# Order of a fused attention and feed-forward kernel: the first 24 heads' output transposes planned after the reciprocals of the sums

## The chip, the cores and the metric

One core of a Trainium2 chip runs the kernel. The metric is the device time of one execution in microseconds (us). The engines are TensorE (PE, its weight loads apart as PEld), VectorE (DVE), ScalarE (ACT), GpSimd (POOL) and SyncE (SP), which issues most of the transfers. Products are made in fp32 or in fp32r, a form of fp32 that the engine takes in one go.

## The reference

Four batches of 12 heads, 448 positions and 64 columns go through attention with a soft cap; the heads' outputs side by side are normalised and go through a feed-forward block with a residual:

```python
scores = scale * np.matmul(q, k.transpose(0, 1, 3, 2))
scores = cap * np.tanh(scores / cap)
scores = scores - np.max(scores, axis=-1, keepdims=True)
attn = np.exp(scores)
attn = attn / (np.sum(attn, axis=-1, keepdims=True) + 1e-09)
return np.matmul(attn, v).astype(np.float32)
...
mu = np.mean(x, axis=-1, keepdims=True)
var = np.mean((x - mu) ** 2, axis=-1, keepdims=True)
xn = (x - mu) / np.sqrt(var + 1e-06) * g_ln
ch = np.maximum(xn @ w_ch1, 0.0) @ w_ch2
return (x + ch).astype(np.float32)
```

## The kernel before, in words

The kernel doesn't write its instructions in the order in which they run. It describes the work as operations (`add`), each with an engine, an assumed cost, the buffers that it reads and writes and a due time. From the reads and writes `Order.add` makes the dependencies. `Order.emit` then plays the program through with the assumed costs: whenever an engine is free it takes, of the operations whose dependencies are met and whose buffers can be had, the one due first, gives it its buffers and writes its instructions. What comes out is a fixed list of instructions for each engine. On the chip every engine goes through its list in order, and its waits follow from the tiles that an instruction really touches; what was only named in `reads` orders the list and makes no wait on the chip.

PSUM has eight banks in four tiles of two banks (named `two_225` to `two_228` in the program; `two` in the profile). A score block of the first heads takes a whole tile, everything else takes one bank of it. Which tile a thing gets is settled by the same play-through, so another order also means other tiles.

Heads come in quads of four (`quad`, L498); the first 24 heads (`LEAD`) are six quads, and the feed-forward work of their tokens only begins when 12 heads are done. A quad is made of these parts:

- Scores, L723: key blocks of 128 against 448 queries, two heads at a time, one in each half of the array's rows (64*128). ACT takes the tanh (L768) and, for three blocks together, the exponential (L776). The last 64 keys are L749 (64*64), their exponential L784.
- Values, L552: the exponentials times V, two heads side by side in columns (128*64), into the accumulators `pos`, one bank for each pair of heads; L559 (64*64) adds the last keys.
- Sums of the exponentials: DVE adds key blocks (L575, L577) and PE sums over partitions with a matrix of ones (L636, L640, 128*32).
- The `pos` are copied to SBUF, the `ot` tiles (L603 through `copy`: L611 on DVE for the first eight heads, L609 on ACT after them), and so are the sums (`ss`, L656).
- `finish` (L647): PE transposes the sums (L662, four of 128x128), DVE adds a small number and takes the reciprocal (L665, L668, tile `r`). PE transposes the outputs (L676): four token tiles, two transposes each, each tile in a bank `pf`. DVE multiplies each by the reciprocals into the token layout (L686), which frees the bank.

After 12 heads, tokens are normalised (L858 to L891), transposed (L899), rounded into a high and a low part (L904 on ACT, L908 on DVE), and the feed-forward products begin (L1019 to L1021 and L1048 to L1050, fp32r, whole array); from some 490 us on the remaining tokens follow in blocks of 512 (L1237 to L1240, L1330 to L1332).

In the kernel before, the transposes L676 name only the two `ot` tiles, so they can be planned as soon as those are copied; the multiplies name `pf` and `r`.

Of the kernel before, what the change touches and what calls it, by code (L numbers as in the profile page):

```python
# [33 lines left out]
LEAD = 24  # L34
# [113 lines left out]
class Order:  # L148
# [9 lines left out]
    def add(self, engines, fn, reads=(), writes=(), allocs=(), due=0.0, dma=0, after=(), lag=0.0):  # L158
        op = Op()
        (op.engine, op.cost), = engines.items()  # L160
        op.fn, op.due, op.dma, op.lag, op.seq = fn, due, dma, lag, len(self.ops)
        deps = set(after)
        for k in reads:
            deps.update(self.writer.get(k, ()))
        for k in writes:
            deps.update(self.writer.get(k, ()))
            deps.update(self.readers.get(k, ()))
        for k in writes:
            self.writer[k], self.readers[k] = [op], []
        for k in reads:  # L170
            self.readers.setdefault(k, []).append(op)
        deps.discard(op)
        op.left, op.outs, op.ready, op.end, op.wait, op.after = len(deps), [], 0.0, None, None, deps
        for d in deps:
            d.outs.append(op)
        bufs = {k[0] if isinstance(k, tuple) else k: 0 for k in (*reads, *writes, *allocs)}
        op.bufs = [b for b in bufs if isinstance(b, Buf)]
        for b in op.bufs:
            self.wide += b.wide and not b.users
            b.users += 1  # L180
            op.ready = max(op.ready, b.since)
        self.ops.append(op)
        return op
# [196 lines left out]
class Program:  # L380
# [25 lines left out]
    def buf(self, pool, tag, shape, dtype, bufs=1):  # L406
        size = 1
        for x in shape[1:]:
            size *= x
        kinds, tags = (GENERAL_KINDS, GENERAL_TAGS) if self.general else (KINDS, TAGS)  # L410
        if tag in tags:
            kind, n = tags[tag]
            self.limits[pool, tag] = n
            bufs, size = kinds[kind]
        else:
            kind = tag
        self.places[pool, kind] = bufs
        b = Buf(pool, kind, tag, shape, dtype)
        self.sizes[pool, kind] = max(size, self.sizes.get((pool, kind), 0))
        return b  # L420
# [226 lines left out]
    def finish(self, i, pairs, ps, due, late):  # L647


        nc, add, buf = self.nc, self.add, self.buf  # L650
        b, h0 = divmod(i, H)
        part = HEADS[-(i < FRONT)]
        due += PLAN["fin"] if h0 + GROUP < H else 0
        ss, d0 = self.out_tile("ss", i, late)
        add({part["ss"]: dict(A=ACTP(S), V=VEC2(S))[part["ss"]]}, lambda e: self.copy(
            e, ss.ap[:, d0:d0 + S], ps.ap[:, :S]), reads=[ps], writes=[(ss, 0)], due=due)  # L656
        pr = buf("ps", "f", [128, 512], F32)
        r = buf("small", "r", [128, NK + 1, GROUP], F32, 2)

        def turn(e):  # L660
            for j in range(NK + 1):
                nc.tensor.transpose(pr.ap[:, j * 128:j * 128 + 128], ss.ap[:, j * 128:j * 128 + 128], self.ident)  # L662

        add({"T": 440}, turn, reads=[(ss, 0), (ss, 2)], writes=[pr], due=due)
        add({"V": 210}, lambda e: nc.vector.tensor_scalar(  # L665
            r.ap, pr.ap.rearrange("p (j c x) -> p j c x", j=NK + 1, c=GROUP)[:, :, :, 0], self.eps, None,
            op0=ALU.add), reads=[pr], writes=[r], due=due)
        add({"V": 220}, lambda e: nc.vector.reciprocal(r.ap, r.ap), writes=[r], due=due)  # L668
        W = GROUP * D
        cols = slice(h0 * D, h0 * D + W)  # L670
        for j, tl, p in self.token_tiles(b):
            pf = buf("ps", "f", [128, 512], F32)

            def turn(e, j=j, pf=pf):
                for c, ot in enumerate(pairs):
                    nc.tensor.transpose(pf.ap[:, c * 128:c * 128 + 128], ot.ap[:, j * 128:j * 128 + 128], self.ident)  # L676

            add({"T": len(pairs) * 110}, turn, reads=[(o, x) for o in pairs for x in (0, 2)] + [r] * self.general, writes=[pf], due=due)
            m = p.stop - p.start
            rows = lambda ap: ap.rearrange("p (h d) -> p h d", d=D)  # L680
            if tl < NA:
                writes, dst = [(self.home(tl)[0], tl, h0)], lambda tl=tl, p=p: self.x(tl)[p, cols]
            else:
                st = buf("att", "stage", [128, W], F32)
                writes, dst = [st], lambda st=st, p=p: st.ap[p]
            add({"V": VEC2(W)}, lambda e, j=j, p=p, m=m, dst=dst, pf=pf: nc.vector.tensor_tensor(  # L686
                out=rows(dst()), in0=rows(pf.ap[p, :W]), in1=r.ap[p, j].unsqueeze(2).to_broadcast([m, GROUP, D]),
                op=ALU.mult), reads=[pf, r], writes=writes, due=due)
            if tl >= NA:
                add({"V": 330}, lambda e, dst=dst, tl=tl, p=p: nc.vector.bn_stats(  # L690
                    self.stats.ap[p, tl % SLOTS, h0 // GROUP], dst()), reads=writes,
                    writes=[(self.stats, tl % SLOTS, h0 // GROUP, p.start)], due=due)
                add({"S": 550}, lambda e, dst=dst, tl=tl, p=p: nc.sync.dma_start(out=self.xd[tl][p, cols], in_=dst()),
                    reads=writes, writes=[("xd", tl, (h0, p.start))], due=due, dma=128 * W * 4)
# [883 lines left out]
```

## Time and profile before

| | |
|---|---|
| three runs | 857.07, 857.84 and 858.79 us, median 857.84 |
| the profiled execution | 857.77 us, of which its span 856.0 us |
| mean granted TensorE clock | 0.998 |
| busy share of the span | PE 99%, PEld 83%, DVE 82%, ACT 60%, POOL 18% |
| chain that ended last | PE 95%, ACT 2%, DVE 1% |

The span goes from the first to the last instruction. A PE row of the timeline gives the start of a stretch of like instructions, its length, and how many there are; an fp32 product in a part of the array counts as two instructions there. The ends of matmuls are modelled and overlap the next stretch, so what a stretch costs is read from its start to the start of the next one.

### The profile page before, as it was taken

How to read it: one execution, taken by the hardware profiler on the slowest of the kernel's cores; microseconds unless marked ns; L12 is line 12 of the kernel's file. 1: busy time of each engine (PE TensorE's matmuls, PEld its weight loads, DVE VectorE, ACT ScalarE, POOL GpSimd, SP SyncE). 2: the span in 40 equal slices, each digit the busy share in tenths (PEclk: the TensorE clock that was granted, in tenths of full speed). 3: DMA queues.
4: the chain of work that ended last, by engine and by line, in shares of the span. 5: the costliest groups of instructions: out<-in, count | busy, mean ns of one | idle time of the engine just before them, and what ended most of it. 6: DMA issues, size and time to landing. Idle time of an engine off the chain costs nothing.

```text
span 856.0 us, 12856 instructions
## 1 busy us (share of the span) xinstructions
PE 845.8 (99%) x4700; PEld 706.4 (83%) x4700; DVE 701.7 (82%) x1157; ACT 511.9 (60%) x795; POOL 152.1 (18%) x198
## 2 busy tenths in 40 slices
PE   8999999999999999999999999999999999999997
PEld 5344477979879799799799989998988998999897
DVE  2689798878789878787689878888888888788896
ACT  6887877644654647354436646756575666566550
POOL 0134231111112111111110001223113212312210
PEclk9999999999999999999999999999999999999999
DMA  9597766665675774654562344798878888787984
GB/s 230 138 251 212 197 179 176 186 204 161 184 221 167 221 210 168 184 169 128 179 254 102 102 143 83 164 180 156 169 159 155 165 169 159 139 191 157 181 220 152
DMA packets 55579, 148.96 MB, mean 174 GB/s; under 512 B 7378, under 2 KB 20178, under 8 KB 55506
## 3 DMA queue, kind: packets, MB, share of 16 engines
q1 hardware_dynamic: 41328, 113.43, 44.8%
q0 software_dynamic: 12096, 33.04, 22.8%
q10 hardware_dynamic: 2082, 1.58, 0.6%
q8 instruction: 39, 0.64, 0.3%
q14 instruction: 34, 0.28, 0.1%
HBM read 87.46 MB, written 60.56 MB: 173 GB/s over the span
## 4 chain that ended last, share of the span: by engine, by line
PE 95%; ACT 2%; DVE 1%; issue 0%; POOL 0%; DVEq 0%; ACTq 0%
PE two L1237 7%; PE two L1330 7%; PE two L1240 7%; PE two L1332 7%; PE two L1331 7%; PE two L1238 7%; PE two L1019 6%; PE two L1048 6%; PE two L1050 6%; PE two L1049 6%; PE two L552 6%; PE two L1021 6%; PE two L1020 6%; PE two L723 6%; PE two L676 1%; PE two L636 1%
## 5 line engine op out<-in xcount | busy, mean ns | idle before, releaser
L1347 POOL DMA_DIRECT2D out_dram<-x x84 | 73.4, 998 | 314.6 <-ACT x L1338 227.2
L1338 ACT ACTIVATE x<-two 128x384 f32<-128x384 f32 x168 | 79.6, 487 | 35.6 <-PE two L1332 27.0
L1237 PE MATMUL two<-X,q 128*128 128x512 f32 x252 | 98.9, 392 | 1.2 <-ACT y L1254 1.2
L1019 PE MATMUL two<-hA,q 128*128 128x384 f32 x288 | 99.8, 347 | 0.0
L1240 PE MATMUL two<-X,q 128*128 128x512 f32 x252 | 98.8, 392 | 0.0
L1238 PE MATMUL two<-X,q 128*128 128x512 f32 x252 | 98.6, 391 | 0.0
L1342 DVE TENSOR_TENSOR x<-two,x 128x384 f32<-128x384 f32 x144 | 76.9, 552 | 26.3 <-PE two L1332 22.7
L1048 PE MATMUL two<-w,hh 128*128 128x384 f32 x288 | 98.3, 341 | 0.0
L1050 PE MATMUL two<-w,hl 128*128 128x384 f32 x288 | 97.2, 337 | 0.0
L1049 PE MATMUL two<-w,hh 128*128 128x384 f32 x288 | 97.1, 337 | 0.0
L1021 PE MATMUL two<-hA,q 128*128 128x384 f32 x288 | 96.9, 337 | 0.0
L1020 PE MATMUL two<-lA,q 128*128 128x384 f32 x288 | 96.8, 336 | 0.0
L951 POOL TENSOR_SCALAR raw<-raw 128x768 f32<-128x768 f32 x48 | 49.5, 1031 | 227.9 <-ACT c L947 213.6
L1330 PE MATMUL two<-w,hop 128*128 128x384 f32 x264 | 89.1, 338 | 0.0
L1332 PE MATMUL two<-w,hop 128*128 128x384 f32 x264 | 88.9, 337 | 0.0
L1331 PE MATMUL two<-w,hop 128*128 128x384 f32 x264 | 88.9, 337 | 0.0
L768 ACT ACTIVATE e<-two,sc 128x448 f32<-128x448 f32 (+1 forms) x108 | 75.0, 758 | 20.1 <-PE two L723 20.1
L1053 DVE TENSOR_TENSOR x<-two,x 128x384 f32<-128x384 f32 x144 | 76.2, 548 | 12.4 <-PE two L1050 12.1
L488 ACT ACTIVATE w<-c 128x768 fp32r<-128x768 f32 x38 | 32.1, 845 | 60.3 <-DVE c L956 22.9
L1019 PEld LDWEIGHTS two<-hA,q 128*128 128x128 f32 x288 | 54.1, 188 | 10.9 <-issue 7.1
L776 ACT ACTIVATE e<-e,capt 128x1344 f32<-128x1344 f32 (+1 forms) x35 | 61.1, 1770 | 0.3
L552 PE MATMUL two<-e,v 128*64 128x448 f32 x288 | 59.2, 547 | 1.1 <-ACT e L776 0.8
(179 smaller groups left out, 1852.1 us busy)
## 6 DMA issues: line engine op xcount, KB each, us to landing
raw<-in_w_dram SPq DMA_DIRECT2D x48, 768.0 KB, 5.0
out_dram<-x POOLq DMA_DIRECT2D x84, 384.0 KB, 7.2
kept<-c SPq DMA_DIRECT2D x47, 384.0 KB, 5.5
d<-in_kq_dram SPq DMA_DIRECT2D x48, 224.0 KB, 5.7
d<-kept SPq DMA_DIRECT2D x23, 384.0 KB, 3.2
c<-kept SPq DMA_DIRECT2D x23, 384.0 KB, 7.4
v<-in_v_dram SPq DMA_DIRECT2D x24, 227.5 KB, 5.8
x<-out_dram SPq DMA_DIRECT2D x13, 384.0 KB, 5.1
```

The costliest lines, as they stand in the source:

```text
L1019: nc.tensor.matmul(ps.ap[:, :n], lhsT=w1h.ap[:, wc], rhs=xh.ap[:, c], start=(c == 0), stop=False)
L1020: nc.tensor.matmul(ps.ap[:, :n], lhsT=w1h.ap[:, wc], rhs=xl.ap[:, c], start=False, stop=False)
L1021: nc.tensor.matmul(ps.ap[:, :n], lhsT=w1l.ap[:, wc], rhs=xh.ap[:, c], start=False, stop=(c == CC - 1))
L1048: nc.tensor.matmul(o, lhsT=h[0].ap[:, mc], rhs=w[0].ap[:, hc], start=(f == 0), stop=False)
L1049: nc.tensor.matmul(o, lhsT=h[0].ap[:, mc], rhs=w[1].ap[:, hc], start=False, stop=False)
L1050: nc.tensor.matmul(o, lhsT=h[1].ap[:, mc], rhs=w[0].ap[:, hc], start=False, stop=(f == last))
L1237: nc.tensor.matmul(ps.ap, lhsT=wh.ap[:, wc], rhs=xs[c].ap[:, 0], start=start and c == 0, **o)
L1238: nc.tensor.matmul(ps.ap, lhsT=wh.ap[:, wc], rhs=xs[c].ap[:, 1], start=False, **o)
L1240: nc.tensor.matmul(ps.ap, lhsT=wl.ap[:, wc], rhs=xs[c].ap[:, 0], start=False, **o)
L1330: nc.tensor.matmul(o, lhsT=hh.ap[:, mc], rhs=wh.ap, start=begin, stop=False, **skip)
L1331: nc.tensor.matmul(o, lhsT=hh.ap[:, mc], rhs=wl.ap, start=False, stop=False, **skip)
L1332: nc.tensor.matmul(o, lhsT=hl.ap[:, mc], rhs=wh.ap, start=False, stop=True, **skip)
```

## The change

One list of reads: for the quads with `i < LEAD` (the first 24 heads, the six quads from 0 to 20) the transposes L676 now also name `r`, so that the plan holds them until the reciprocal L668 is done. For the other heads nothing is named anew. The general version of the kernel (not run with these inputs) already named `r` and goes on doing so.

```diff
-            add({"T": len(pairs) * 110}, turn, reads=[(o, x) for o in pairs for x in (0, 2)] + [r] * self.general, writes=[pf], due=due)
+            add({"T": len(pairs) * 110}, turn, reads=[(o, x) for o in pairs for x in (0, 2)] + ([r] if self.general else [r] if i < LEAD else []), writes=[pf], due=due)
```

The transposes read no element of `r`, so no wait for it arises on the chip; the play-through gives other lists. Both programs have the same instructions, 4308 matmuls on PE's list among them, in another order.

PE, the end of the first quad (`b_231`, `b_233` are its `ot` tiles, `b_235` its sums), before:

```order
L662 MATMUL two_227<-ident,b_235 128x128 x4
L676 MATMUL two_227<-ident,b_231 128x128
L676 MATMUL two_227<-ident,b_233 128x128
L676 MATMUL two_226<-ident,b_231 128x128
L676 MATMUL two_226<-ident,b_233 128x128
```

and now:

```order
L662 MATMUL two_227<-ident,b_235 128x128 x4
L749 MATMUL two_226<-d_245 64x448 x2
L749 MATMUL two_226<-d_254 64x448 x2
L723 MATMUL two_228<-d_299 128x448 x2
L552 MATMUL two_227<-e_296,v_251 64x448 x6
L676 MATMUL two_225<-ident,b_231 128x128
L676 MATMUL two_225<-ident,b_233 128x128
```

The eight transposes L676 stood right behind the four of the sums; now the last scores of the next quad, a score block of the quad after it and half of the next quad's values come between.

DVE, the same place (`r_362` is the first quad's reciprocals, `d_245` the second quad's sum over key blocks, `e_248` exponentials), before:

```order
L665 TENSOR_SCALAR r_362<-two_227,eps 128x16
L668 RECIPROCAL r_362<-r_362 128x16
L686 TENSOR_TENSOR x_373<-two_227,r_362 128x256
L686 TENSOR_TENSOR x_373<-two_226,r_362 128x256 x2
L686 TENSOR_TENSOR x_386<-two_227,r_362 64x256
L858 BN_STATS sx_389<-x_373 128x6 x3
L575 TENSOR_TENSOR d_245<-e_248 128x896
L577 TENSOR_TENSOR d_245<-d_245,e_248 128x896
```

and now:

```order
L665 TENSOR_SCALAR r_362<-two_227,eps 128x16
L668 RECIPROCAL r_362<-r_362 128x16
L575 TENSOR_TENSOR d_245<-e_248 128x896
L577 TENSOR_TENSOR d_245<-d_245,e_248 128x896
L686 TENSOR_TENSOR x_399<-two_225,r_362 128x256 x2
L686 TENSOR_TENSOR x_399<-two_226,r_362 128x256
L686 TENSOR_TENSOR x_403<-two_226,r_362 64x256
L858 BN_STATS sx_405<-x_399 128x6 x3
```

The multiplies, which free the banks of the transposes, moved behind the two sums L575 and L577 of the next quad.

PE, the end of the third quad (`d_77` holds its last exponentials, `d_291` keys and queries of a later quad), before:

```order
L559 MATMUL two_226<-d_77,v_229 64x448
L723 MATMUL two_225<-d_291 128x448 x2
L723 MATMUL two_228<-d_291 128x448 x2
L723 MATMUL two_227<-d_291 128x448 x2
L676 MATMUL two_226<-ident,b_231 128x128
L676 MATMUL two_226<-ident,b_233 128x128
```

and now:

```order
L559 MATMUL two_227<-d_77,v_229 64x448
L723 MATMUL two_225<-d_291 128x448 x2
L723 MATMUL two_226<-d_291 128x448 x2
L723 MATMUL two_227<-d_291 128x448 x2
L662 MATMUL two_228<-ident,b_235 128x128 x4
L749 MATMUL two_225<-d_282 64x448 x2
```

Both accumulators of the quad now lie in one tile, `two_227`, where one lay in `two_226`; the third score block still goes into `two_227`, and behind the three blocks stand the transposes of the sums instead of those of the outputs.

## Rows read from the trace of the kernel before

**Rows 1.** The page, busy time of the engines (share of the span) and instructions.

```profile
PE 845.8 (99%) x4700; PEld 706.4 (83%) x4700; DVE 701.7 (82%) x1157; ACT 511.9 (60%) x795; POOL 152.1 (18%) x198
```

**Rows 2.** Timeline of PE: start us, length us, engine, line, tiles, shape, count.

```profile
25.37 2.53 PE L723 MATMUL two<-d 64*128 64x448 f32 x12
27.83 0.66 PE L662 MATMUL two<-ident,b 128*128 128x128 f32 x4
28.32 1.09 PE L676 MATMUL two<-ident,b 128*128 128x128 f32 x8
29.34 0.98 PE L749 MATMUL two<-d 64*64 64x448 f32 x8
30.25 2.48 PE L552 MATMUL two<-e,v 128*64 128x448 f32 x12
32.66 1.77 PE L723 MATMUL two<-d 64*128 64x448 f32 x8
34.36 2.48 PE L552 MATMUL two<-e,v 128*64 128x448 f32 x12
36.77 1.02 PE L723 MATMUL two<-d 64*128 64x448 f32 x4
37.72 0.96 PE L636 MATMUL two<-d,ones 128*32 128x448 f32 x8
...
39.36 0.98 PE L559 MATMUL two<-d,v 64*64 64x448 f32 x8
```

**Rows 3.** Timeline of PE, six fp32r products of the feed-forward between two score stretches.

```profile
85.98 0.44 PE L1019 MATMUL two<-hA,q 128*128 128x384 f32 x1
86.26 0.34 PE L1020 MATMUL two<-lA,q 128*128 128x384 f32 x1
86.44 0.33 PE L1021 MATMUL two<-hA,q 128*128 128x384 f32 x1
...
87.22 1.77 PE L723 MATMUL two<-d 64*128 64x448 f32 x8
```

**Rows 4.** Timeline of PE at the end of the third quad.

```profile
55.60 2.52 PE L723 MATMUL two<-d 64*128 64x448 f32 x10
58.29 1.02 PE L723 MATMUL two<-d 64*128 64x448 f32 x2 [0.16 <-ACT b L609]
59.23 1.09 PE L676 MATMUL two<-ident,b 128*128 128x128 f32 x8
60.26 1.24 PE L749 MATMUL two<-d 64*64 64x448 f32 x8
61.42 1.02 PE L723 MATMUL two<-d 64*128 64x448 f32 x4
```

**Rows 5.** Timeline of PE at the end of the fourth quad.

```profile
68.89 1.13 PE L636 MATMUL two<-d,ones 128*32 128x448 f32 x6
...
71.08 0.98 PE L559 MATMUL two<-d,v 64*64 64x448 f32 x8
...
72.80 2.53 PE L723 MATMUL two<-d 64*128 64x448 f32 x12
76.12 1.07 PE L899 MATMUL two<-ident,xn 128*128 128x128 f32 x6 [0.79 <-DVE lA L908]
```

**Rows 6.** Timeline of ACT at the end of the third quad.

```profile
55.26 2.54 ACT L776 ACTIVATE e<-e,capt 128x2688 f32<-128x2688 f32 x1
57.70 0.96 ACT L609 ACTIVATE b<-two 128x448 f32<-128x448 f32 x2
```

**Rows 7.** Timeline of DVE, first and fourth quad.

```profile
29.31 1.41 DVE L686 TENSOR_TENSOR x<-two,r 128x256 f32<-128x256 f32 x4
...
31.88 2.52 DVE L575 TENSOR_TENSOR d<-e 128x896 f32<-128x896 f32 x1 [0.17 <-ACT e L776]
34.43 1.09 DVE L577 TENSOR_TENSOR d<-d,e 128x896 f32<-128x896 f32 x1
...
68.31 1.09 DVE L577 TENSOR_TENSOR d<-d,e 128x896 f32<-128x896 f32 x1
```

**Rows 8.** Timeline of POOL at the end of the first quad.

```profile
31.66 1.80 POOL L951 TENSOR_SCALAR raw<-raw 128x768 f32<-128x768 f32 x2
```

## The prediction

> **What bounds the kernel.** I read the page's busy shares first. PE is busy for 845.8 of 856.0 us [rows 1], so only two things can move the time: what PE's instructions cost in their order, and the places where PE waits. I then read PE's timeline through the 24 heads, from the start of each stretch to the start of the next. It is strikingly regular: the same stretch takes the same time wherever it stands, unless something is late. Twelve score instructions take 2.46 us (25.37 to 27.83), eight take 1.70 and four 0.95; L749 takes 0.91, twelve value instructions 2.41, eight transposes L676 1.02 and four transposes of the sums 0.49 [rows 2]. Last I looked for stretches that take longer than that. There are four, and most of their excess is not shown as idle time, because the modelled end of a matmul covers it:
>
> - At the end of the third quad the twelve score instructions take 3.63 us (55.60 to 59.23) instead of 2.46: 1.17 us too long, for which the row names ACT's copy L609 [rows 2, 4].
> - Right behind, L749 takes 1.16 us (60.26 to 61.42) instead of 0.91: 0.25 us [rows 2, 4].
> - The sums of the fourth quad (L636 and L640) take 2.19 us (68.89 to 71.08) against 1.64 in a quad that doesn't wait (37.72 to 39.36): 0.55 us. DVE's L577, which makes their operand, only starts at 68.31 [rows 2, 5, 7].
> - The scores from 72.80 to 76.12 take 3.32 us instead of 2.46: 0.86 us, for which the row names DVE's L908 [rows 2, 5].
>
> Together PE loses 2.83 us at these places. Before 27.83 us it loses more, in filling the pipe, but both orders are the same up to there.
>
> **What the change does.** On the chip nothing waits for the reciprocals that did not before: the transposes read no element of `r`. The change acts through the lists alone. No instruction is added or removed on any engine, DMAs included. PE's list differs from the end of the first quad (27.83 us) on; from some 240 us on the kinds of stretches and their lengths are the same in both, but for the tiles. So I price two terms, and neither grows with the length of the kernel.
>
> **Term 1: more changes of the array's shape.** Counted in the two lists up to the blocks of 512 tokens, the stretches of one shape (64*128, 64*64, 128*64, 128*32 or 128*128) rise from 134 to 142. The eight more are one of scores, one of values, one with fp32r products and five of transposes alone. Each stretch has a cost of its own beside its instructions:
>
> - Scores: four more instructions cost 0.75 us (1.70 less 0.95), so a stretch of four (0.95) holds 0.20 us of its own [rows 2].
> - Values: all stretches of this kind in the rows hold twelve instructions, so this is not separated; I take the 0.20 us of the scores.
> - fp32r: six products take 1.24 us (85.98 to 87.22), while in the middle one takes 0.18 (86.26 to 86.44), say 0.175. Six make 1.05, and 0.19 us is left [rows 3].
> - Transposes alone: eight take 1.02 us and four more, in one stretch with them, 0.49, so the stretch's own share can be as little as 0.04 us [rows 2]. The upper bound is the 0.20 of the others. I take the middle, 0.12, since these rows are near to neither end.
>
> The sum is 0.20 + 0.20 + 0.19 + 5 x 0.12 = 1.19 us more, with bounds of 0.8 and 1.6. The Trainium skill has a rule that speaks against such a change: "TensorEngine Tiling (Array Packing)", section Tiling Modes, says that changing the tiling mode drains the engine. "TensorE: Matmul & The Clock Gate", Part 2, puts the drain of the array at some 128 cycles, which gives an estimate of 0.05 us at 2.4 GHz and 0.4 us for eight; the rows say three times as much, and I go by the rows.
>
> **Term 2: PE's waits.** I go through the new list with the durations above.
>
> - Third quad. The block that waits goes into `two_227`. Before, it needed only the first of the two copies L609 (57.70, two in 0.96 us), which stood behind the exponential at 55.26 [rows 6]. Now both accumulators lie in that tile, so it needs both copies, which alone is half a microsecond worse. But the quad's last scores now stand ahead of L636 and L640 instead of behind them, so the exponential can start earlier, by an estimate of 1.3 us from the 1.64 of the two [rows 2]. Net I expect 0.65 us of the 1.17 to stay (bounds 0 and 1.2), and the 0.25 behind it to go.
> - Fourth quad, sums: DVE's list now has L577 of this quad ahead of the chain of the normalisation that delayed it. I expect the 0.55 us to go.
> - Fourth quad, scores: the transposes L899 were two lots of six and waited for L908. Now four of them come in threes, with scores and values between, so the 0.86 us go.
> - New waits. The output transposes now need banks while scores use them, and the values behind them go into a tile that the transposes have just filled, so PE waits for the first multiply. I put 0.2 us there. The threes of L899 share `two_228` with the sums' transposes and wait for DVE at one or two points, 0.35 us. Nothing in the trace before shows either; they are bounded by 0 and by the largest wait of this kind, 0.86 each.
>
> Waits after the change: 0.65 + 0.2 + 0.35 = 1.2 us, 1.63 fewer than 2.83. Other queues: SP's and POOL's lists change in the same stretch (loads of keys and queries, of weights, and the zeroing of pads move by a few places). I cost them at nothing because none of the four waits names a DMA or POOL; if a load came late, its wait would come on top of all this.
>
> **Sum.** The profiled execution took 857.77 us, 0.07 under the median of 857.84. 857.77 + 1.19 - 1.63 = **857.3** us. That is 0.06% under the median, and a measurement of this kernel can tell about 0.2% (1.7 us) from no change, so I forecast no change that can be told.
>
> **Rivals.**
>
> *Slower: the multiplies come too late.* DVE now does L575 and L577 before the four multiplies that free the transposes' banks. L575 waits for the exponential and here took 2.52 us from 31.88, L577 then ended at 35.52, and four multiplies take 1.41 us [rows 7]; so two banks are free at 36.2 and all at 36.9 us. PE, in the new order, comes to the second score block, which needs the first two, at 27.83 + 0.53 + 0.91 + 0.95 + 2.41 + 1.02 + 2.41 + 0.75 = 36.8 us, and to L636, which needs the others, at 37.8. That leaves 0.6 to 0.9 us of slack. L575 can lose 1.43 us: it took 2.52 where L577 took 1.09 for the same size, just while POOL ran L951 (31.66, 1.80 us for two) [rows 7, 8]. The Trainium skill's "SBUF — State Buffer", section Who interferes with whom, says that a DVE instruction with two SBUF inputs contends with a GpSimd instruction that reads SBUF; this row fits it. If a second such loss hits each of four quads, PE waits about 4 x (1.43 - 0.7) = 2.9 us more: 860.2 us. The rival decides from 2.2 us over my forecast on, that is from multiplies that are some 1.25 us later than I walk in four quads. For it speaks how full DVE is; against it, that DVE still ends before PE arrives in each quad that I walked. Chance 0.16.
>
> *Waits stay as large.* ACT and DVE are shared as before, so other waits of 2.8 us may replace the old ones. Then only term 1 is left: 857.77 + 1.2 = 859.0 us. Chance 0.22, within 0.2%.
>
> *Faster: all waits go.* Then 857.77 + 0.8 - 2.8 = 855.8 us with the lower bound of term 1, and 856.2 with its value. For it: three of the four waits have a cause that the new lists take away. Against it: the accumulators' copies remain on ACT behind an exponential. Chance 0.13.
>
> *It doesn't do what it says*, since no wait for `r` exists on the chip: that is so in any case, and the lists are then all there is.
>
> **How the numbers follow.** My forecast has 0.49. With 0.22 for unchanged waits and 0.13 and 0.16 for the ends, faster by over 0.2% (below 856.1) gets 0.13, slower by over 0.2% (above 859.6) 0.16, and between lies 0.71. The range goes from 856.0 to 859.9 us: down to nearly the end of the faster case, up past the case of unchanged waits and into the lower part of the slower one, with a tenth left out on each side.
>
> **What would show it.** In the profile after, PE's stretches should have the same lengths as in the rows above, with L676 alone between values; the score stretch at the end of the third quad should take 2.5 to 3.2 us, not 3.63; the sums of the fourth quad 1.64; no L899 should wait for over half a microsecond. Start of the feed-forward and the stretch from 240 us on should be shifted as a block by under 2 us. I am wrong if PE shows a wait on L686, or on a load, of over a microsecond in several quads, or if the stretch behind 240 us changes its length.

## The result, and the profile after

The changed kernel took 862.87 us, median of 6 executions (860.32 to 863.89), beside 857.74 for the kernel before on the same chip (6 executions, 857.07 to 859.61): a ratio of 1.0053 [1.0041, 1.0065]. It is slower by half a per cent, 5 us where the prediction had none, and lies outside its range.

The profiled execution is the shortest of the six, 860.32 us (span 858.5). The page shows PE as before, against [rows 1]:

```profile
PE 845.8 (99%) x4700; PEld 705.8 (82%) x4700; DVE 703.9 (82%) x1157; ACT 512.3 (60%) x795; POOL 152.0 (18%) x198
```

The busy time of PE tells nothing, since the modelled end of a matmul covers waits. So I read PE's timeline again from start to start, at the places of [rows 4, 5] (columns as in [rows 2]):

```profile
55.13 3.22 PE L723 MATMUL two<-d 64*128 64x448 f32 x12
58.28 0.66 PE L662 MATMUL two<-ident,b 128*128 128x128 f32 x4
...
61.49 1.09 PE L676 MATMUL two<-ident,b 128*128 128x128 f32 x8
64.11 2.48 PE L552 MATMUL two<-e,v 128*64 128x448 f32 x12 [1.53 <-DVE x L686]
...
69.88 0.96 PE L636 MATMUL two<-d,ones 128*32 128x448 f32 x8
...
71.52 0.98 PE L559 MATMUL two<-d,v 64*64 64x448 f32 x8
...
74.14 1.19 PE L899 MATMUL two<-ident,xn 128*128 128x128 f32 x6
75.25 1.02 PE L723 MATMUL two<-d 64*128 64x448 f32 x4
...
78.18 1.02 PE L723 MATMUL two<-d 64*128 64x448 f32 x4
80.29 0.55 PE L899 MATMUL two<-ident,xn 128*128 128x128 f32 x3 [1.09 <-DVE r L665]
```

- Third quad, scores: 3.15 us (55.13 to 58.28) for twelve instead of 2.46, so 0.69 us too long. Predicted 0.65.
- Third quad, values: the eight L676 should take 1.02 us [rows 2] and take 2.62 (61.49 to 64.11). 1.60 us are lost before L552, on DVE's multiply L686. Predicted 0.2.
- Fourth quad, sums: 1.64 us (69.88 to 71.52). The 0.55 us of before are gone, as predicted.
- Fourth quad, L899: six take 1.11 us (74.14 to 75.25) where the same six take 0.81 in the kernel before (71.99 to 72.80), so 0.30; and four scores in front of the last three take 2.11 us (78.18 to 80.29) instead of 0.95: 1.16 us, on DVE's L665. Predicted 0.35 for both.

These are 3.75 us of waits, against 2.83 before (3.0 with one of 0.2 us behind the fourth quad's scores that the prediction's list left out). The rest of this execution can be added up. The values' stretch that starts at 19.46 us before starts at 19.22 here; the last matmul starts at 851.56 instead of 850.04. So between those two points PE lost 1.76 us more: 0.7 of it in the listed waits, and 1.0 is left for the stretches themselves and whatever else differs. Behind the last matmul the span has 6.9 us instead of 6.0. That makes -0.24 + 1.76 + 1.0 = 2.5 of the 2.55 us between the two profiled executions (860.32 less 857.77).

So this profile accounts for 2.5 us, not the 5 of the medians. Of 16 executions of the changed kernel, all told, seven took 859.9 to 860.9 us, all with a mean granted clock of 0.998 or 0.999, and nine took 862.3 to 863.9, seven of them at 0.995 to 0.997. What happens in those nine had to be found.

**Who is late in the third quad.** DVE's timeline of the changed kernel:

```profile
59.62 1.50 DVE L956 SCALAR_TENSOR_TENSOR c<-c,raw 128x768 int32<-128x768 int32 x1
61.05 0.24 DVE L668 RECIPROCAL r<-r 128x16 f32<-128x16 f32 x1
62.08 1.65 DVE L495 TENSOR_TENSOR w<-c,w 128x768 fp32r<-128x768 f32 x1 [0.79 <-POOL w L492]
63.65 1.40 DVE L686 TENSOR_TENSOR x<-two,r 128x256 f32<-128x256 f32 x4
```

and POOL's:

```profile
59.26 1.06 POOL L948 TENSOR_SCALAR c<-raw 128x768 f32<-128x768 f32 x1 [0.43 <-DMA kept<-c]
61.21 0.83 POOL L492 TENSOR_SCALAR w<-c 128x768 fp32r<-128x768 f32 x1 [0.89 <-DVE c L956]
```

The reciprocal L668 is ready at 61.29, but the multiplies stand on DVE's list behind L495, which splits the next block of weights (`w_71`). L495 waits for POOL's copy L492, and that one stands on POOL's list behind L948, which waits for a store (`kept<-c`) to land. The kernel before had the multiplies ahead of that split:

```profile
59.71 1.41 DVE L686 TENSOR_TENSOR x<-two,r 128x256 f32<-128x256 f32 x4 [0.78 <-PE two L676]
...
71.08 0.95 DVE L495 TENSOR_TENSOR w<-c,w 128x768 fp32r<-128x768 f32 x1
```

The transposes moved behind the reciprocal, so the multiplies came later in the order, and the split, which had stood 11 us behind them, now stands ahead. Through it PE hangs on DVE, DVE on POOL, and POOL, whose copy stands behind L948, on a store. In this profile the store isn't what comes last: the row of L492 names DVE's L956 (0.89 us), which took 1.50 us with L948 beside it.

### The profile page after: what moved, and what is told of

Same layout as the page of the kernel before. It is cut to its first block, busy times and chain, and to the rows that moved or that the text cites. A ratio compares the mean times of both kernels' runs of the same rounds, so it can differ in the third digit from the quotient of the medians.

```text
span 858.5 us, 12838 instructions
## 1 busy us (share of the span) xinstructions
PE 845.8 (99%) x4700; PEld 705.8 (82%) x4700; DVE 703.9 (82%) x1157; ACT 512.3 (60%) x795; POOL 152.0 (18%) x198
## 3 DMA queue, kind: packets, MB, share of 16 engines
q10 hardware_dynamic: 2082, 1.58, 0.6%
## 4 chain that ended last, share of the span: by engine, by line
PE 94%; DVE 2%; ACT 2%; issue 1%; POOL 0%; ACTq 0%
PE two L1237 7%; PE two L1330 7%; PE two L1240 7%; PE two L1332 7%; PE two L1331 7%; PE two L1238 7%; PE two L1019 6%; PE two L1048 6%; PE two L1050 6%; PE two L552 6%; PE two L1049 6%; PE two L1021 6%; PE two L1020 6%; PE two L723 5%; PE two L676 1%; PE two L636 1%
## 5 line engine op out<-in xcount | busy, mean ns | idle before, releaser
L951 POOL TENSOR_SCALAR raw<-raw 128x768 f32<-128x768 f32 x48 | 50.4, 1051 | 223.3 <-ACT c L947 208.9
L552 PE MATMUL two<-e,v 128*64 128x448 f32 x288 | 59.4, 548 | 2.5 <-DVE x L686 1.5
```

## Experiments

All moves of single operations use one edit. The planner runs as it does; when an operation listed in `HOLD` comes to be written, it is kept back until the named ones have been written (the numbers count the operations in the order in which the program describes them). Of the edit, this is the line where it takes hold. Tiles and all other places stay; only its place on its own engine's list moves:

```
-                run(o, e)
+                self.send(run, o, e)
```

**The changed kernel again.**

> The changed kernel as it is, once more, to see a second execution in a profile beside more times. In the first profile (860.3 us, the fastest of its six runs) PE ends 1.5 us later than before; the median is 862.9. Theory 1 (the new lists' waits on DVE in the first 24 heads vary from run to run): a profiled execution of 862 to 864 us shows the values behind the transposes of the third quad, or L899 behind L665 in the fourth, waiting 2 to 4 us more in total than the 1.6 and 1.2 us of the first profile, and PE's stretch from 240 us on unchanged in length. Theory 2 (a stretch behind 240 us, or the start, varies): the first 24 heads are as in the first profile within 0.5 us and the 2.5 us lie in the filling of the pipe before 27 us or behind 240 us.

861.58 us (860.16 to 863.11), ratio 1.0044 [1.0031, 1.0057]. The profile, of the shortest execution, has L552 waiting 3.33 us (1.53 above), with DVE's L495 waiting 3.13 us for POOL, and POOL's L948 3.35 us for its store; the fourth quad's waits are the same 0.30 and 1.17. The wait at 64 us varies with the execution, by 1.8 us. This execution is as short as the first all the same: PE loses 1.74 us more between the fill and the last matmul, but the values start at 18.17 instead of 19.22, and 0.8 us less lie behind the last matmul.

**The third quad's split behind the multiplies.** `HOLD = {800: (143, 145, 147, 149)}`: L495 of `w_71` behind the four L686.

> One edit on DVE's list of the changed kernel: in the third quad the split of a weight (L495, which waits for POOL) goes behind the four multiplies L686 instead of ahead of them. Everything else keeps its place and tile. Theory 1: the 1.6 us wait of the values at 64 us goes almost wholly, and the median falls by 1.5 us or more, to 861.4 or lower (more if it is this wait that varies). Theory 2: the wait goes in the profile, and the median falls by 1.5 us and no more. If the wait only moves (the sums of the fourth quad become late instead), the median falls by under 0.7 us.

861.25 us (858.78 to 863.51), ratio 1.0036 [1.0024, 1.0048]. The wait of L552 is gone (61.38 to 62.41 for the eight L676, 1.03 us), but the time isn't: PE gets earlier to the fourth quad and waits there, 1.15 us in the sums and 1.76 before L899, where the changed kernel lost 0.30:

```profile
73.57 0.33 PE L899 MATMUL two<-ident,xn 128*128 128x128 f32 x1
74.39 0.33 PE L899 MATMUL two<-ident,xn 128*128 128x128 f32 x1 [0.49 <-DVE xn L891]
75.55 0.66 PE L899 MATMUL two<-ident,xn 128*128 128x128 f32 x4 [0.83 <-DVE xn L891]
```

The median is 0.3 us under that of the repeat, as expected for a wait that only moves. DVE is behind in both quads; one move passes the wait on.

**Both quads.** As before, and `821: (226,), 264: (226,), 849: (226,)`: in the fourth quad L665, and the two L908 ahead of it, come ahead of the split of `w_72`, of L577 and of L954.

> As the run before, and in the fourth quad the reciprocals' first step L665 goes ahead of L495, L577 and L954 on DVE's list, so that the bank of the sums' transposes is free for L899. Theory 1: both DVE waits go, the median falls by 2.6 us at least, to 860.3 or lower, and to some 858 if these are the waits that vary. Theory 2: the median falls by 2.6 us at most and stays at or above 860.2.

859.26 us (858.71 to 861.87), ratio 1.0023 [1.0013, 1.0033]: 2.3 us less than the changed kernel. Both large waits are gone:

```profile
60.62 1.09 PE L676 MATMUL two<-ident,b 128*128 128x128 f32 x8
61.65 2.48 PE L552 MATMUL two<-e,v 128*64 128x448 f32 x12
...
77.46 0.55 PE L899 MATMUL two<-ident,xn 128*128 128x128 f32 x3
77.94 1.02 PE L723 MATMUL two<-d 64*128 64x448 f32 x4
...
86.69 0.66 PE L676 MATMUL two<-ident,b 128*128 128x128 f32 x4 [1.19 <-DVE lA L908]
```

What is left of waits is 3.5 us (0.69, 1.10, 0.32 and a new one of 1.37 at 86.69), only 0.25 less than in the changed kernel's first profile: most of the waiting has been passed on, in smaller pieces. From the fill to the last matmul this profile lost 1.53 us more than the kernel before, where the changed kernel's first lost 1.76. So the 2.3 us of the medians are not what this profile gains over a short execution of the changed kernel; the larger part must lie in the long ones.

**The changed kernel once more.**

> A third look at the changed kernel, for the spread between profiled executions. Theory 1: any time over 861.5 us goes with longer waits on DVE between 27 and 110 us. Theory 2: it goes with a longer stretch elsewhere.

859.93 us, L552's excess 1.49, L899's 1.86 at 80 us. So the second wait varies too, and the rows show with what. In the first profile DVE's L954 started ahead of POOL's L948 (78.10 and 78.22) and took 0.95 us, L948 1.58; here L948 was ahead (77.39 and 77.46), and L954 took 1.64 us, L948 0.90. So it is in all nine profiles, of this list and of those with one move, in which the two overlap: whichever starts later takes 0.7 to 0.8 us more.

**POOL's store out of the chain.** `HOLD = {816: (799,)}`: POOL's L948, which waits for the store, behind L492.

> The changed kernel with one place moved on POOL's list alone: the copy into c_66 (L948), which waits for the store of the buffer before it, comes behind the copy w_71 (L492) instead of ahead of it. Theory 3 (the time was lost in a chain: store kept<-c lands, POOL L948, POOL L492, DVE L495, DVE L686, PE L552, so that the store's landing sets the third quad's values): the wait of L552 on DVE's L686, 1.5 to 3.4 us in the three profiles of the changed kernel, falls under 1 us, the median by 1.5 to 2.5 us to 859.0 to 860.3 us, and the spread of the runs gets smaller. Rival (DVE itself has too much to do ahead of L686, whatever POOL waits for): the wait stays at 1.2 us or more and the median falls by at most 0.7 us.

861.03 us (856.97 to 863.32), ratio 1.0037 [1.0022, 1.0052]. The theory fell as it was put, and the rival's two numbers came out. The wait of L552 did get shorter, 1.29 us lost, less than in any profile of the changed kernel, and no store is in the chain any more:

```profile
61.02 0.83 POOL L492 TENSOR_SCALAR w<-c 128x768 fp32r<-128x768 f32 x1 [2.06 <-DVE c L956]
```

But the median is only 0.55 us lower and the executions lie in two groups, six at 857.0 to 859.9 us with a clock of 0.998 or more and six at 862.1 to 863.3 with 0.995 to 0.997. L956, which POOL's L492 waits for here, took 0.95 us without L948 beside it. In the changed kernel's profiles it took 1.50 to 1.57 with L948 beside it, and L492 waited for it last; only where L552 waited longest did the store land so late that L492 waited for L948 instead. So L948 accounts for what L552 waits beyond 1.2 to 1.3 us, by its store or by slowing L956; that much comes from the split's place on DVE; and the long executions come from something else.

**POOL's and DVE's moves together.**

> The move on POOL's list together with the moves on DVE's list of the two runs before (w_71's split behind the third quad's multiplies; r's multiply of the fourth quad ahead of w_72's split, the normalisation L577 and the copy L954). Theory 3: what is left above the kernel before is the shape changes, 1.2 us, and about half a us of waits: 858.3 to 859.2 us. If the store's landing was not what varied, it stays where the DVE moves alone stood, 859.3 us, within 0.4.

859.43 us (858.33 to 861.27), ratio 1.002 [1.0011, 1.0029], within 0.2 us of the DVE moves alone: with the split behind the multiplies the store doesn't matter. None of the 22 executions of these two kernels has a mean clock under 0.998.

**Moves in the kernel before.** `HOLD = {164: (214,), 264: (173,)}`: the normalisation's short operations behind L577, the next L577 behind the L908 that the fourth quad's scores wait for.

> The kernel before with two places moved on DVE's list: the normalisation that fills the short waits comes behind the ones that PE's fourth-quad sums and scores wait for. The prediction's second term said that the waits of the kernel before at 69 to 76 us cost 0.55 and 0.86 us of its time. If so, 856.0 to 856.6 us, 1.0 to 1.5 us under the kernel before, and the two waits are gone from the profile. If such waits are taken back by a later wait (of a load or of DVE), within 0.4 us of the kernel before.

856.20 us (855.81 to 858.67), ratio 0.9985 [0.9974, 0.9996]: 1.4 us under the kernel before, and the best of all kernels here. Both waits of [rows 5] are gone, 1.64 us for the sums and 2.45 for twelve scores:

```profile
67.79 0.96 PE L636 MATMUL two<-d,ones 128*32 128x448 f32 x8
...
69.43 0.98 PE L559 MATMUL two<-d,v 64*64 64x448 f32 x8
...
71.15 2.53 PE L723 MATMUL two<-d 64*128 64x448 f32 x12
73.60 0.87 PE L899 MATMUL two<-ident,xn 128*128 128x128 f32 x6
```

About half of it is taken back at once, in 0.8 us of waits that end at 79.5 and 82.1 us; from the fill to 230 us the profile is only 0.8 us ahead. Why the median gains 1.4 (0.3 to 2.2 by the interval) is not shown.

**The kernel before, profiled again.**

> The kernel before, looked at a second time. Theory 3: its waits between 27 and 110 us are again the four of the first profile, 2.8 us within 0.4, since no copy of POOL that waits for a store stands ahead of what PE waits for. If its waits change by over 1 us with the execution, what varies is not the order of the changed kernel.

857.56 us, with 1.16, 0.25, 0.54 and 0.86 us (and again the 0.2): the four waits of the first profile to a hundredth. From the fill to the last L749 (407.39 us in the first profile, 406.18 here) the two agree to 0.02 us; behind it they differ by 0.8. So the waits that vary in the first 24 heads are those of the changed order, as far as two profiles tell.

**The fourth quad's moves alone.** `HOLD = {821: (226,), 264: (226,), 849: (226,)}`.

> The changed kernel with the fourth quad's part of the DVE moves alone: r's multiply (L665) and the sum of the low parts before it come ahead of w_72's split, the normalisation L577 and the copy L954; the third quad stays as changed. In half of their executions the changed kernel and the one with the POOL move take 2 to 4 us more than in the others, at a granted clock of 0.995 to 0.997 over the span instead of 0.998 to 1.0. Theory 4 (the waits of PE at 74 to 81 us, on the sum of the low parts and on r, grow in these executions until the clock of TensorE falls for some us): no execution at 0.997 or lower, and a median at 859.6 to 860.6 us. Rival (what grows is the third quad's wait of L552 at 64 us): as the changed kernel, 861 to 862 us, half of the executions long, with a low clock.

860.71 us (859.65 to 864.80), ratio 1.005 [1.003, 1.007]. The median is 0.1 us above what theory 4 allowed, and two of six executions have a low clock, 863.83 us at 0.996 and 864.80 at 0.994. So the fourth quad's wait can't be the only one that brings it.

**A longer wait in the fourth quad.** `HOLD = {226: (850,)}`: L665 behind one more L956.

> The changed kernel with the wait of L899 on DVE's L665 at 80 us made longer: L665 comes behind the sum L956 of the weights as well, 1.4 us of DVE. Theory 4: the wait becomes some 2.5 us, the median rises by more than those 1.4 us, to 863 us or more, since most executions get the low clock, and if the profile falls in one of them, it shows after which wait the clock falls. Rival (the low clock comes from another place): plus 1.4 us and no more, 862.5 to 863 us, as many executions at 0.997 and lower as the changed kernel has.

863.55 us (861.78 to 864.54), three of five executions at 0.994 or 0.995, and the profiled one (863.83) among them. PE's timeline, and then a table of stretches (us; PE, PEld, DVE, ACT, POOL busy; granted clock; DMA share; GB/s):

```profile
81.64 0.90 PE L899 MATMUL two<-ident,xn 128*128 128x128 f32 x3 [2.66 <-DVE r L665]
...
84.26 4.40 PE L552 MATMUL two<-e,v 128*64 128x448 f32 x12
88.59 0.55 PE L899 MATMUL two<-ident,xn 128*128 128x128 f32 x3
```

```profile
80.00:81.00 1.00, 0.00 (x0) 0.00 (x0) 1.00 (x3) 1.00 (x1) 0.28 (x1) 1.00 1.13 254
81.00:82.00 1.00, 0.36 (x2) 0.37 (x3) 0.96 (x4) 0.51 (x1) 0.00 (x0) 0.68 1.05 237
82.00:83.00 1.00, 1.00 (x5) 0.65 (x5) 1.00 (x2) 0.42 (x1) 0.00 (x0) 0.50 1.33 212
...
88.00:89.00 1.00, 1.00 (x7) 0.31 (x3) 0.00 (x0) 0.00 (x0) 0.00 (x0) 0.91 0.94 369
```

Here is what a long execution can pay. PE waits 2.66 us for L665, the granted clock falls from 1.0 to 0.5 (from 2.4 to 1.2 GHz) as it goes on, and stays there to 88.2. Twelve values take 4.33 us (84.26 to 88.59) instead of 2.41.

**The changed kernel and the POOL move, profiled for a long execution.**

> The changed kernel, looked at once more, for a profile of one of its long executions (862 us and more). Theory 4: such a profile shows a stretch with a granted clock under 1 behind the waits at 74 to 81 us. Rival: behind the wait at 64 us, or at another place. A short execution (860 us) tells nothing.

860.24 us, no low clock in the first 24 heads, waits of 0.70, 1.68, 0.30 and 1.87 us: a short execution, and nothing to tell.

> The changed kernel with the POOL move, looked at once more, for the same reason: 6 of its 12 executions took 862 to 863.3 us, at a clock of 0.995 to 0.997. Theory 4: in a long one the clock falls behind the waits at 74 to 81 us. A short one tells nothing.

862.17 us. The table by stretches has the clock at 0.5 from some 81.7 to 85.1 us, behind a wait of 1.82 us:

```profile
80.50 0.55 PE L899 MATMUL two<-ident,xn 128*128 128x128 f32 x3 [1.82 <-DVE r L665]
80.98 1.24 PE L723 MATMUL two<-d 64*128 64x448 f32 x4
82.15 3.90 PE L552 MATMUL two<-e,v 128*64 128x448 f32 x12
```

```profile
81.00:82.00 1.00, 1.00 (x5) 0.28 (x4) 1.00 (x4) 1.00 (x3) 0.00 (x0) 0.83 1.03 233
...
85.00:86.00 1.00, 1.00 (x7) 0.16 (x3) 0.97 (x2) 0.00 (x0) 0.00 (x0) 0.97 0.94 378
```

It costs 1.42 us in the values and 0.2 in the scores. So theory 4 holds for this kernel, at this wait. Yet the mean clock of this execution is 0.998. In every profile here the clock also falls to 0.5 behind the last matmul (in the kernel before from 853.4 us to the end at 856.0), which by itself gives a mean of 0.998 or 0.999. So a mean of 0.998 leaves room for up to some 4.3 us at half speed (0.0025 x 2 x 858): it excludes a stretch like that of the run before, 6.8 us, and not one like this, 3.4 us.

**A longer wait in the third quad.** The fourth quad's moves with `799: (817,)`: POOL's copy of `w_71` behind one more L951.

> The changed kernel with the fourth quad's DVE moves, and the third quad's wait made longer: on POOL's list the copy w_71 (L492), for which DVE's split L495 waits ahead of the multiplies L686, comes behind one more operation (L951, 0.9 to 1.5 us). Theory 5 (a long wait of PE lets the clock fall wherever it stands, at 64 us as at 80 us): the wait of L552 becomes 3 to 4 us, most executions are at 0.997 or lower, the median is 863 us or more, and a profile of such an execution has its stretch under 1 between 64 and 75 us. Rival (only the wait at 80 us does it): 861.5 to 862.5 us, no execution at 0.997 or lower.

860.74 us (859.99 to 862.87), one of five executions at 0.996. The edit missed: the wait stayed at 1.62 us, because POOL's copy waits for DVE's L956 anyway and L951 fits in front of it. This run tells nothing of theory 5.

**The changed kernel and the fourth quad's moves, for the same purpose.**

> The changed kernel, looked at again for a profile of a long execution. Theories 4 and 5: if it takes 862 us or more, the profile has a stretch at a granted clock of 0.5 behind the wait at 80 us (or at 64 us), 3 to 7 us long, which costs 1.5 to 3.5 us.

862.53 us: a long execution of the changed kernel itself. Its PE, DVE and POOL:

```profile
61.36 1.09 PE L676 MATMUL two<-ident,b 128*128 128x128 f32 x8
65.65 4.75 PE L552 MATMUL two<-e,v 128*64 128x448 f32 x12 [3.19 <-DVE x L686]
70.33 1.55 PE L723 MATMUL two<-d 64*128 64x448 f32 x4
71.81 2.48 PE L552 MATMUL two<-e,v 128*64 128x448 f32 x12
...
83.16 0.55 PE L899 MATMUL two<-ident,xn 128*128 128x128 f32 x3
```

```profile
63.64 1.62 DVE L495 TENSOR_TENSOR w<-c,w 128x768 fp32r<-128x768 f32 x1 [2.31 <-POOL w L492]
65.19 1.40 DVE L686 TENSOR_TENSOR x<-two,r 128x256 f32<-128x256 f32 x4
```

```profile
61.91 0.90 POOL L948 TENSOR_SCALAR c<-raw 128x768 f32<-128x768 f32 x1 [3.21 <-DMA kept<-c]
62.78 0.83 POOL L492 TENSOR_SCALAR w<-c 128x768 fp32r<-128x768 f32 x1
```

and its clock (columns as above):

```profile
63.00:64.00 1.00, 0.00 (x0) 0.00 (x0) 0.36 (x1) 1.00 (x2) 1.00 (x2) 1.00 1.07 237
64.00:65.00 1.00, 0.00 (x0) 0.00 (x0) 1.00 (x1) 1.00 (x2) 0.62 (x3) 0.80 1.04 232
65.00:66.00 1.00, 0.35 (x2) 0.30 (x4) 1.00 (x4) 1.00 (x2) 0.00 (x0) 0.50 1.17 273
...
70.00:71.00 1.00, 1.00 (x4) 0.51 (x4) 0.85 (x1) 0.00 (x0) 0.92 (x1) 0.50 0.06 25
71.00:72.00 1.00, 1.00 (x6) 0.19 (x4) 0.33 (x2) 0.04 (x1) 0.61 (x1) 0.78 0.03 12
```

The whole chain is in these rows. The store lands late, POOL's L948 waits 3.21 us for it, DVE's L495 2.31 us for POOL, PE 3.19 us for L686, and while PE stands still the clock goes to 0.5 and stays there until some 71.4. The values take 4.68 us (65.65 to 70.33) instead of 2.41 and four scores 1.48 instead of 0.95: 2.8 us on top of 3.27 of waiting (61.36 to 65.65, less 1.02). In return DVE has caught up and L899 at 83.16 waits for nothing. From the fill (19.09) to the last matmul (854.79) PE lost 5.1 us more than in the kernel before, 3.4 more than in the changed kernel's first profile. The Trainium skill, "TensorE: Matmul & The Clock Gate", Part 1, says that the clock is set by how busy the engine has been recently, and names a full and a half rate as its two states. The rows agree, with 1.00 and 0.50 and a mean of the two where it changes; but in the first repeat of this kernel the clock stayed at 1.00 through 3.33 us without a matmul.

> The changed kernel once more, with the expectation of the look before: a long execution has a stretch at a granted clock of 0.5 behind the wait at 80 us or at 64 us, 3 to 7 us long.

859.91 us, short: waits of 2.06 and 1.86 us, and no low clock there.

> The changed kernel with the fourth quad's DVE moves, looked at again: 2 of its 6 executions took 863.8 and 864.8 us at 0.996 and 0.994. Theory 5: a long one has its stretch at 0.5 behind the third quad's wait at 64 us. Rival: behind the waits at 83 to 88 us that the moves left. A short one tells nothing.

860.69 us, short: the third quad's 1.69 us, and 1.35 at 88.6 us, no low clock there. That the low clock of this kernel's two long executions comes from its wait at 64 us is likely after what the changed kernel showed, but no profile of one shows it.

## Why the prediction was wrong

**Term 1, the changes of shape: right in size.** It was put at 1.19 us with bounds of 0.8 and 1.6. Between fill and last L749, where the two profiles of the kernel before agree to 0.02 us, the first profile after lost 1.94 us more (19.22 to 409.09 against 19.46 to 407.39), and 1.2 are left when the listed waits are taken off on both sides; with the DVE moves in both quads 1.68, and again 1.2 are left. Up to the last matmul 1.0 and 1.1 are left, but there the profiles of one kernel differ by 0.7. This is worked out as a remainder; no run changed the number of stretches alone. One of the prices that the prediction borrowed can be read in the kernel before after all:

```profile
45.15 4.73 PE L552 MATMUL two<-e,v 128*64 128x448 f32 x24
49.81 1.77 PE L723 MATMUL two<-d 64*128 64x448 f32 x8
```

A stretch of 24 value instructions takes 4.66 us, two of twelve 4.82, so one has 0.16 us of its own where 0.20 was taken.

**Term 2, the waits that go: right.** The 0.55 us of the sums and the 0.25 and 0.86 us of the scores went as said, and the third quad's scores kept 0.69 where 0.65 stood (the exponential started 1.4 us earlier, 53.88 instead of 55.26, where an estimate of 1.3 stood). That two of these waits were real time in the kernel before is borne out by the DVE moves in it, which take them away: 0.8 us in the profile, after other waits took some of it back, and 1.4 at the median.

**Term 2, the new waits: the step that failed.** "I put 0.2 us there" and "0.35 us" were mis-sized: the first was 1.5 to 3.4 us in six profiles, the second 1.5 to 2.2 in five of them. Even the lesser sum, 3.06 us in the first profile, is 2.5 above the 0.55 of the prediction, and without it the short executions would have come out near the forecast. For the first, I walked DVE's list only where the multiplies stood behind L575 and L577, in the first quad, and took the other quads for the same. In the third another operation came ahead of them, the split of `w_71`, and with it POOL. For the second I read which engine PE waits for, but did not add up what DVE still has to do ahead of L665: L956 (0.95 us), L891 (2.94), L575 (1.77), L495, L577, L954 and two L908 in one row, with hardly a gap from 70.8 to 80.0 us.

**Other queues at nothing: wrong, by its own words.** "None of the four waits names a DMA or POOL" was true of the order before and says nothing of the new one, where POOL's copy for the split has lost its slack and stands behind a store. The store came last in two of six profiles and made the longest waits, 3.3 and 3.4 us.

**What was left out altogether: the clock.** The prediction let a wait cost its own length. In three profiles a stretch at half speed goes with one: 2.8 us for 6.8 us of it in the long execution of the changed kernel, 1.6 us for 3.4 in the POOL move's, and 6.8 us of it again in the run with the longer wait. In that long execution PE lost 3.4 us more than in the first profile, of which 3.0 add up: 2.8 by the clock and 1.7 by the longer wait, less 1.5 given back in the fourth quad. Whether this is what parts the others of the nine long executions (median 862.7 us) from the seven short ones (860.2) is not shown. It is likely for the six more whose mean clock is 0.995 to 0.997, none of them profiled. For the two at 0.998 and 0.999 it is hardly enough: the one at 0.999 took 863.89 us, the longest of all, and has room for at most some 2.6 us at half speed, the program's end included. In the two kernels with the moves in both quads no execution of 22 had a mean under 0.998, which excludes the long stretches only; in the kernel before 5 of 70 had a mean of 0.997 or less.

**The rival "the multiplies come too late"** had the right engine and the right wait, but another mechanism (L575 beside POOL, in four quads); that its 860.2 us is also the median of the short executions is luck. "Waits stay as large" with 859.0 is close to what the DVE moves in both quads give, 859.3, but that is another kernel. Of the prediction's signs, "no L899 should wait for over half a microsecond" failed at 80.29 us (1.09), and "a wait on L686 of over a microsecond in several quads" came in one quad only.

**Open.** Three things: what makes the store land late (of the changed kernel's six profiles, two have SP's issue of the four loads L513 at 57 us take 5.0 and 5.1 us, and there POOL's L948 waits 3.35 and 3.21 us for the store; in the other four it takes 2.5 to 2.8, and the wait is 0.3 to 1.0; which of the two brings the other is not shown), why the clock falls after some waits and not after others of the same length; and what else moves a whole execution by some us: the first values start anywhere from 18.2 to 19.5 us whatever the kernel, the stretch behind 407 us differs by up to 1.2 us between profiles, and the kernel with the moves in both quads took from 858.71 to 861.87 us with no mean clock under 0.998.

## What to carry to other kernels

Where a new order comes from a planner, walk each engine's list at every place at which PE will wait, not at one and by analogy, and for each operation that now stands ahead of the releasing one ask what it waits for, down to the stores. A wait of two or three microseconds on TensorE is to be priced with what the clock may take behind it, and a median can move by more than a profile of a short execution shows: look at the mean clock of every execution before explaining the profile that one happens to have. The mean clock shows long stretches at half speed only. And a full DVE gives a wait that a moved operation mostly hands on: with the moves in both quads 3.5 us of 3.75 were still there, in pieces of 1.4 us and less.

## What the runs showed that I had not expected

- The clock fell behind a wait of only 1.82 us in one execution (with 1.2 us lost at another some 17 us earlier), while it stayed at 1.0 through one of 3.33 us in another execution of nearly the same list.
- The stretch at half speed lasted 3.4 to 6.8 us, though PE was at work again 1.0 us after it began at the latest (65.65 against some 64.6), and in one execution before it began (80.50 against 81.7).
- Two operations moved on DVE's list of the kernel before are worth more (1.4 us at the median) than the whole change was expected to move (0.5 us).
